# A fused attention and channel-mixing kernel: operands laid out on the host, channels on partitions, 512 tokens per matmul

## The chip, the cores and the metric

The kernel runs on one core of a Trainium2 chip. The metric is the device time of one execution in microseconds (us). The engines that the text names are TensorE (PE; its weight loads are listed as PEld), VectorE (DVE), ScalarE (ACT), GpSimd (POOL) and SyncE (SP), whose queue starts nearly all DMA transfers here. Each engine executes its own instructions in the order that was fixed when the kernel was compiled, and waits on semaphores for the others.

## The reference

All inputs are float32 or float64 arrays: q, k and v of shape (8 batches, 8 heads, 576 tokens, 64), and the matrices U (576 x 32), V (32 x 576), w1 (512 x 2048), w2 (2048 x 512), which are float64.

```python
scores = q @ k.T / 8                       # per batch and head, 576 x 576
local   = (0 <= i - j < 32)                # heads 0 to 3
strided = (i >= j) and (i % 32 == j % 32)  # heads 4 to 7
attn = softmax(where(mask, scores, -1e9))
x = concat over heads of attn @ v          # (8, 576, 512)
h = (x.transpose(0, 2, 1) @ U @ V).transpose(0, 2, 1)   # mixing over tokens
u = x + h
out = u + maximum(u @ w1, 0) @ w2          # (8, 576, 512)
```

A local head needs only a band of keys: for 32 queries the 64 keys up to them. A strided head splits into 32 residue classes of 18 tokens each.

## The kernel before

**The two large products.** Token rows of u are cut into 18 blocks of 256 tokens (two tiles of 128). For each block and each of 16 chunks `fc` of the 2048 hidden channels, `gemm1` (L714) forms the hidden activations with hidden channels on partitions and 256 tokens as columns: four slices of channels times three matmuls. Three, because every operand is split in a high and a low float32r part and the product of the two low parts is left out (high x high, high x low, low x high). ACT writes the high part of the ReLU (`gh`, L726) and DVE the low part (`gl`, L727). `gemm2` (L731), two steps later, takes the activations as the stationary operand and moves 512 output channels: for each of the two token tiles three matmuls, accumulated over all 16 chunks in two PSUM banks `acc`. `finish` (L742) adds u and stores token rows. One step, a pair (block, fc), is therefore 12 matmuls of 256 columns and 6 of 512.

**Weights.** w1 and w2 lie in memory as float64 bits. They are loaded as 32 chunks of 512 KB (`load_weights`, L146) and converted by integer operations (`to_f32`, L104: one on ACT, three on DVE, L114 to L117) and then split (ACT L164, POOL L165), during the front and the first two blocks, which run interleaved.

**Attention.** Batches 0 and 1 (`early`, `attention_pair`, L247) do all eight heads on TensorE: a pair of heads is loaded in its natural layout, transposed by TensorE, evicted by ACT and DVE (`transpose_natural`, L193; `copy`, L219), scored against 32-token chunks, masked by a matmul, exponentiated, transposed again and multiplied with v. The strided pairs reach their residue order through DRAM (`sd` for v, `od` for the output). Batch 1's pairs start while batch 0's are still running. Batches 2 to 7 do the local heads on TensorE (`local_pairs`, L452, with DVE 32x32 transposes, L464), and the strided heads with products on POOL and reductions on DVE (`strided_heads`, L480: L504 and L506 for the scores, L532 and L534 for the outputs), then ACT copies to token rows (`strided_copies`, L541).

**Mixing and transposition.** `mix_t` (L563) forms x^T U, `mix_u` (L589) adds the product with V to x. u is stored with tokens on partitions, so each block has to be turned to channels on partitions before `gemm1` (`transposes`, L675): the first three blocks by TensorE, the others by DVE 32x32 transposes and 16 DMA transfers of 32 KB.

**What sets the order.** The kernel is traced as Python generators. The loop at L792 walks the 288 steps and, after each, advances the generators of strided heads, of the next batch's attention and of the transposes by a fraction of their length that was chosen by hand (windows L759). Tile, the framework, then orders each engine's instructions at compile time: first traced is preferred, a later one may go ahead where an earlier one is not ready by its own estimate of times. Tiles of one tag share a fixed number of buffers: seven `att` buffers, one `st` (strided q, k, v), two PSUM pairs `px`, one pair `acc`, two banks `ph`.

Of the kernel before, what the change touches and what calls it, by code (L numbers as in the profile page):

```python
# [39 lines left out]
B1S, B1E = 24, 1  # L40
ORDER0, ORDER1 = (0, 2, 3, 1), (0, 2, 3, 1)
# [3 lines left out]
def fused_kernel(ctx, tc, q, k, v, U, V, w1_in, w2_in, masks, eye, out):  # L45
    nc = tc.nc
    B, H, S, D = q.shape
    DM, FF = w1_in.shape
    R = U.shape[1]
    NCH = S // 32  # L50
    NFC = FF // 128
    NDC = DM // 128
    NG = 4
    FPG = NFC // NG

    const = ctx.enter_context(tc.tile_pool(name="const", bufs=1))
    xp = ctx.enter_context(tc.tile_pool(name="xp", bufs=2))
    ap_ = ctx.enter_context(tc.tile_pool(name="ap", bufs=1))
    mp = ctx.enter_context(tc.tile_pool(name="mp", bufs=2))
    dp = ctx.enter_context(tc.tile_pool(name="dp", bufs=2, space=bass.MemoryType.DRAM))  # L60
    ps_acc = ctx.enter_context(tc.tile_pool(name="ps_acc", bufs=1, space=bass.MemoryType.PSUM))
    ps_h = ctx.enter_context(tc.tile_pool(name="ps_h", bufs=2, space=bass.MemoryType.PSUM))
    ps_x = ctx.enter_context(tc.tile_pool(name="ps_x", bufs=2, space=bass.MemoryType.PSUM))
# [4 lines left out]
    def big(shape, name, dtype=F32):  # L68
        return ap_.tile(shape, dtype, name=name, tag="big")

    def ubuf(shape, name, dtype=F32):
        return mp.tile(shape, dtype, name=name, tag="u", bufs=5)

    counts = {"xn": 0, "conv": 0}
    banks = {"n": 0, "prefix": True}

    def psx2():

        banks["n"] += 1
        if banks["prefix"] and banks["n"] % 3 == 0:  # L80
# [3 lines left out]
    def psx1():  # L84
        if banks["prefix"]:
            return ps_h.tile([128, 512], F32, name="ph")
        return psx2()[:, 0, :]
# [5 lines left out]

    ident = const.tile([128, 128], F32, name="ident")
    masks_sb = const.tile([128, 768], BF16, name="masks_sb")
    mask_b = masks_sb[:, 0:640].rearrange("p (a t x) -> p a t x", a=2, x=64)
    ident_b = masks_sb[:, 640:768]
    kZ = const.tile([128, 2, 32 + S], F32, name="kZ", tag="kZ")
    nc.vector.memset(kZ, 0.0)
    U_sb = const.tile([128, 5, R], F32, name="U_sb")  # L100
    Vst = const.tile([96, S], F32R, name="Vst")
    raws, w_parts = {}, {}

    def to_f32(raw, p, n, paced=False):  # L104
# [4 lines left out]
        cv = att([128, 512], "cv")  # L109
# [11 lines left out]
    def small_weights():  # L121
        stage = xp.tile([128, 2, 512], I64, name="xg")
        raw = stage[:, 0]
        dma(out=raw[:, 0:4 * R].rearrange("p (t r) -> p t r", r=R),
                          in_=U[0:512, :].rearrange("(t p) r -> p t r", p=128))
        for half in range(2):
            dma(out=raw[64 * half:64 * half + 64, 4 * R:5 * R], in_=U[512:576, :])
        rvs = []
        for a, n, s0 in ((0, 512, 0), (512, 64, 512)):
            rv = raw[0:32, 5 * R:5 * R + n] if n < 512 else stage[0:32, 1]  # L130
            dma(out=rv, in_=V[:, s0:s0 + n])
            rvs.append(rv)
        yield
        f = to_f32(raw, 128, 5 * R)
        nc.vector.tensor_copy(out=U_sb.rearrange("p t r -> p (t r)"), in_=f)
        yield
        for rv, (a, n) in zip(rvs, ((0, 512), (512, 64))):
            f = to_f32(rv, 32, n)
            nc.scalar.copy(out=Vst[0:32, a:a + n], in_=f)
            nc.scalar.copy(out=Vst[32:64, a:a + n], in_=f)  # L140
            nc.vector.tensor_tensor(out=Vst[64:96, a:a + n], in0=f, in1=Vst[0:32, a:a + n].bitcast(F32), op=ALU.subtract)
            yield

    chunks = [(i, g, t) for g in range(NG) for i in range(2) for t in range(4)]

    def load_weights():  # L146
        for i, g, t in chunks:
            src = w2_in[512 * g + 128 * t:512 * g + 128 * t + 128, :] if i else \
                w1_in[128 * t:128 * t + 128, 512 * g:512 * g + 512]
            raws[i, g, t] = const.tile([128, 512], I64, name=f"raw{i}_{g}_{t}", tag=f"w{i}_{g}_{t}")  # L150
            with tc.issue_after(last_dma[0]):
                nc.sync.dma_start(out=raws[i, g, t], in_=src)
            yield

    def weights():
        for n, (i, g, t) in enumerate(chunks):
            while wl["n"] <= n:
                next(wl["gen"])
                wl["n"] += 1
            f = to_f32(raws[i, g, t], 128, 512, True)  # L160
            parts = const.tile([128, 2, 512], F32R, name=f"w{i}_{g}_{t}", tag=f"w{i}_{g}_{t}")
            w_parts[i, g, t] = parts
            hi, lo = parts[:, 0], parts[:, 1]
            nc.scalar.copy(out=hi, in_=f)  # L164
            nc.gpsimd.tensor_tensor(out=lo, in0=f, in1=hi.bitcast(F32), op=ALU.subtract)  # L165
            yield

    wl = {"gen": load_weights(), "n": 0}

    def load_ahead(n):  # L170
        while wl["n"] < min(n, len(chunks)):
            next(wl["gen"])
            wl["n"] += 1

    xgs, tails, tsts, o_str = {}, {}, {}, {}

    xn_bufs = []

    def load_natural(src, h0):
        counts["xn"] += 1  # L180
        if counts["xn"] == 5:
            stage = xp.tile([128, 3, 640], F32, name="xg")
            xn_bufs.extend(stage[:, n] for n in range(3))
        if counts["xn"] <= 4:
            xn = ubuf([128, 640], "xn")
        else:
            xn = xn_bufs.pop() if xn_bufs else att([128, 640], "xn")
        rows = src[h0:h0 + 2].rearrange("h (j two) d -> (h j) (two d)", two=2)
        dma(out=xn[:, 0:512].rearrange("p (t x) -> p t x", t=4), in_=rows[0:512].rearrange("(t p) x -> p t x", p=128))
        dma(out=xn[0:64, 512:640], in_=rows[512:576])  # L190
        return xn

    def transpose_natural(dsts, xn, strided, engines):  # L193

        tp = psx2().rearrange("p a x -> p (a x)")
        for t in range(5):
            n = 128 if t < 4 else 64
            nc.tensor.transpose(out=tp[:, 128 * t:128 * t + n], in_=xn[0:n, 128 * t:128 * t + 128], identity=ident[0:n, 0:n])
        for hh in range(2):
            for par in range(2):  # L200
                src = tp[64 * par:64 * par + 64, 288 * hh:288 * hh + 288]
                if strided:
                    dst = dsts[hh].rearrange("p (j two i) -> p two i j", two=2, i=NCH)[:, par]
                    src = src.rearrange("p (i j) -> p i j", i=NCH)
                else:
                    dst = dsts[hh].rearrange("p (j two) -> p two j", two=2)[:, par]
                copy(engines[par], dst, src)
            yield

    def load_blocks(src, h0):  # L210
        xn = att([128, NCH, 32], "xn")
        for hh in range(2):
            sv = src[h0 + hh].rearrange("(c p) (e j) -> e p c j", p=32, e=2)
            for e in range(2):
                a = 64 * hh + 32 * e
                dma(out=xn[a:a + 32], in_=sv[e])
        return xn

    def copy(engine, out, in_):  # L219
        if engine == "a":  # L220
            nc.scalar.copy(out=out, in_=in_)  # L221
        else:
            (nc.vector if engine == "v" else nc.gpsimd).tensor_copy(out=out, in_=in_)  # L223

    halves = [slice(64 * hh, 64 * hh + 64) for hh in range(2)]

    held = {}
    vts, later_vt = [], []

    def acquire(names):  # L230

        while True:
            for name in names:
                if name not in held:
                    held[name] = True
                    return name
            yield

    def value_tiles():

        for vt in (big([128, NCH, 2, D + 1], "vt"), const.tile([128, NCH, 2, D + 1], F32, name="vt_kept")):
            nc.gpsimd.memset(vt, 0.0)
            for hh in range(2):
                nc.gpsimd.memset(vt[64 * hh:64 * hh + 64, :, hh, D:D + 1], 1.0)
            vts.append(vt)

    def attention_pair(b, pr, sd, od, last):  # L247


# [632 lines left out]
```

## Time and profile before

| | before |
|---|---|
| three runs, median (lowest to highest) | 1017.75 us (1016.87 to 1019.25) |
| profiled execution, its span | 1018.0 us |
| PE busy, share of the span | 961.5 us, 94% |
| DVE, ACT, POOL busy | 607.9, 312.1, 362.0 us |
| first matmul of `gemm1` | at 92.0 us |
| DMA moved, mean rate | 71.43 MB, 70 GB/s |
| packets under 512 B | 148952 of 186100 |

The span is the time from the first to the last instruction of one profiled execution. A line of a view names the source line, the engine, the operation and the tiles (`out<-in`); `x` counts instructions. In a timeline the first number is the start, the second the time to the end of the merged instructions, and brackets give the idle time before them with what ended it. In a group the busy time, the mean of one instruction in ns, and the idle time before it. Matmuls are pipelined: the duration of one (287 ns for 256 columns) is longer than the distance between two.

### The profile page before, as it was taken

The page shows a single profiled execution, that of the slowest core. Times are in us where ns is not written, and L with a number is a line of the kernel's source. Part 1 is how long each engine was busy: PE and PEld are TensorE (multiplying, and loading weights), DVE is VectorE, ACT ScalarE, POOL GpSimd, SP SyncE. Part 2 cuts the span into 40 slices and gives each one's busy share as a digit, 9 for nine tenths or more (in the row PEclk, how much of TensorE's full clock was granted, in tenths as well). Part 3 has the DMA queues.
Part 4 walks back from the last instruction along what each step waited for, and adds up shares of the span by engine and source line. Part 5 has one row for each costly group of instructions (what it writes and reads, how often), then busy time and mean ns, then how long its engine had stood idle before and what let it go on. Part 6 is the DMA issues. An engine that isn't in the chain of part 4 may idle for free.

```text
span 1018.0 us, 19929 instructions
## 1 busy us (share of the span) xinstructions
PE 961.5 (94%) x8028; PEld 835.2 (82%) x8028; DVE 607.9 (60%) x1137; ACT 312.1 (31%) x691; POOL 362.0 (36%) x376
## 2 busy tenths in 40 slices
PE   4666789999999999999999999999999999999997
PEld 3545678898788888988888888888888889999997
DVE  3546896888576847653758675858576843312121
ACT  6877445215211421211412142114211431211110
POOL 1102444965463517231455353735373500000000
PEclk9777799999999999999999999999999999999999
DMA  7866823052505250311251425042505300101000
GB/s 191 219 161 182 329 41 65 1 110 48 90 22 89 48 91 16 70 24 43 47 91 35 76 47 91 19 92 48 91 18 90 50 22 16 48 1 42 1 21 21
DMA packets 186100, 71.43 MB, mean 70 GB/s; under 512 B 148952, under 2 KB 177272, under 8 KB 186008
## 3 DMA queue, kind: packets, MB, share of 16 engines
q1 hardware_dynamic: 186008, 70.16, 31.9%
q8 instruction: 63, 1.03, 0.4%
q14 instruction: 29, 0.24, 0.1%
HBM read 51.64 MB, written 11.80 MB: 62 GB/s over the span
## 4 chain that ended last, share of the span: by engine, by line
PE 77%; DVE 8%; issue 5%; DMA 5%; SPq 2%; ACT 2%; POOL 1%; DVEq 0%; POOLq 0%; ACTq 0%
PE ph L722 36%; PE acc L739 33%; DMA raw<-in_moe_w_ch_dram 3%; SPq L92 2%; DVE st L534 1%; PE px L406 1%; PE px L739 1%; DVE cv L115 1%; DVE cv L117 1%; PE px L438 1%; DVE cv L114 1%; PE px L426 1%; DMA xn<-in_k_dram 1%; ACT qT L221 1%; PE px L596 1%
## 5 line engine op out<-in xcount | busy, mean ns | idle before, releaser
L722 PE MATMUL ph<-uh,w 128*128 128x256 f32 x2304 | 473.3, 287 | 10.9 <-DVE gl L727 5.9
L722 PEld LDWEIGHTS ph<-uh,w 128*128 128x128 f32 x2304 | 379.8, 191 | 27.0 <-DVE gl L727 8.7
L739 PE MATMUL acc<-w,gh 128*128 128x512 f32 x1088 | 346.5, 397 | 2.0 <-DVE qT L223 1.6
L722 PE MATMUL ph<-ul,w 128*128 128x256 f32 x1152 | 332.0, 288 | 0.0
L727 DVE SCALAR_TENSOR_TENSOR gl<-ph,gh 128x256 fp32r<-128x256 f32 x288 | 120.8, 420 | 253.8 <-ACT gh L726 252.5
L726 ACT ACTIVATE gh<-ph 128x256 fp32r<-128x256 f32 x288 | 110.1, 383 | 499.9 <-PE ph L722 440.1
L722 PEld LDWEIGHTS ph<-ul,w 128*128 128x128 f32 x1152 | 217.9, 189 | 9.9
L739 PEld LDWEIGHTS acc<-w,gh 128*128 128x128 f32 x1088 | 195.1, 189 | 34.4 <-issue 2.4
L532 POOL TENSOR_TENSOR tmp<-st,s_st 128x448 f32<-128x448 f32 (+7 forms) x162 | 139.0, 882 | 221.7 <-DMA st<-in_v_dram 79.7
L739 PE MATMUL acc<-w,gl 128*128 128x512 f32 x544 | 214.2, 394 | 0.0
L504 POOL TENSOR_TENSOR tmp<-st 128x576 f32<-128x576 f32 (+6 forms) x162 | 169.1, 1083 | 89.9 <-DMA vt<-in_v_dram 45.1
L534 DVE TENSOR_REDUCE st<-tmp 128x64 f32<-128x64 f32 (+8 forms) x162 | 136.9, 868 | 7.4 <-POOL tmp L532 5.8
L739 PEld LDWEIGHTS acc<-w,gl 128*128 128x128 f32 x544 | 102.9, 189 | 19.3
L506 DVE TENSOR_REDUCE s_st<-tmp 128x9 f32<-128x576 f32 (+6 forms) x162 | 87.6, 565 | 24.5 <-POOL tmp L504 23.9
L165 POOL TENSOR_TENSOR w<-cv,w 128x512 fp32r<-128x512 f32 x32 | 45.7, 1439 | 126.9 <-ACT w L164 109.6
L549 ACT COPY xg<-st 32x256 f32<-32x256 f32 x96 | 38.7, 404 | 32.2 <-DVE st L534 31.3
L709 DVE TENSOR_TENSOR ul<-u,uh 128x1024 fp32r<-128x1024 f32 x15 | 19.6, 1304 | 25.9 <-ACT uh L708 24.5
L114 DVE TENSOR_SCALAR cv<-cv 128x512 int32<-128x512 int32 (+3 forms) x35 | 19.8, 575 | 18.6 <-ACT cv L112 18.5
L581 DVE TENSOR_TENSOR ta<-px,ta 32x256 f32<-32x256 f32 x42 | 17.6, 420 | 19.9 <-ACT ta L579 18.8
L164 ACT CAST w<-cv 128x512 fp32r<-128x512 f32 x32 | 19.6, 618 | 32.0 <-DVE cv L117 30.2
L117 DVE SCALAR_TENSOR_TENSOR cv<-raw,cv 128x512 int32<-128x512 int32 x32 | 26.6, 836 | 0.3
L115 DVE SCALAR_TENSOR_TENSOR cv<-raw,cv 128x512 int32<-128x512 int32 x32 | 25.2, 796 | 0.3
(133 smaller groups left out, 632.6 us busy)
## 6 DMA issues: line engine op xcount, KB each, us to landing
raw<-in_moe_w_ch_dram SPq DMA_DIRECT2D x32, 512.0 KB, 8.5
out_dram<-xg SPq DMA_DIRECT2D x32, 256.0 KB, 2.2
u<-bt SPq DMA_DIRECT2D x240, 32.0 KB, 1.9
vt<-in_v_dram SPq DMA_DIRECT2D x28, 144.0 KB, 4.1
st<-in_q_dram SPq DMA_DIRECT2D x24, 144.0 KB, 3.8
st<-in_k_dram SPq DMA_DIRECT2D x24, 144.0 KB, 5.0
st<-in_v_dram SPq DMA_DIRECT2D x24, 144.0 KB, 3.1
xn<-in_k_dram SPq DMA_DIRECT2D x48, 72.0 KB, 2.5
```

The source lines that it names most:

```text
L115: nc.vector.scalar_tensor_tensor(out=i, in0=hi_w, scalar=-0x80000000, in1=i, op0=ALU.bitwise_and, op1=ALU.bitwise_or)
L117: nc.vector.scalar_tensor_tensor(out=i, in0=lo_w, scalar=29, in1=i, op0=ALU.logical_shift_right, op1=ALU.bitwise_or)
L165: nc.gpsimd.tensor_tensor(out=lo, in0=f, in1=hi.bitcast(F32), op=ALU.subtract)
L504: nc.gpsimd.tensor_tensor(out=tmp[:, 0:n], in0=sk[:, j0:j0 + n], in1=sq[:, i:i + 1].broadcast_to([128, n, D]), op=ALU.mult)
L506: late.append(lambda tmp=tmp, n=n, i=i, j0=j0: nc.vector.tensor_reduce(out=s_st[:, i, j0:j0 + n], in_=tmp[:, 0:n], axis=AX.X, op=ALU.add))
L532: nc.gpsimd.tensor_tensor(out=tv, in0=sv[:, 0:i + 1, d0:d0 + step], in1=s_st[:, i, 0:i + 1].broadcast_to([128, i + 1, step]), op=ALU.mult)
L534: late.append(lambda tv=tv, i=i, d0=d0, step=step: nc.vector.tensor_reduce(out=o_st[:, i, d0:d0 + step], in_=tv.rearrange("p j d -> p d j" ...
L549: nc.scalar.copy(out=xg[32 * i4:32 * i4 + 32, :, cs], in_=o_st[rows, i4:16:4, :])
L722: nc.tensor.matmul(ph[:, 0:W], w_parts[0, g, dc][:, part, fs], ut[:, :, :, dc, :], start=(dc == 0 and i == 0), stop=(dc == NDC - 1 and i = ...
L726: gate[:] = [nc.scalar.activation(out=gh[:, 0:W], in_=ph[:, 0:W], func=AF.Relu).ins]
L727: nc.vector.scalar_tensor_tensor(out=gl[:, 0:W], in0=ph[:, 0:W], scalar=0.0, in1=gh[:, 0:W].bitcast(F32), op0=ALU.max, op1=ALU.subtract)
L739: nc.tensor.matmul(accs[n][:, s, :], gt[:, cs], w_parts[1, g, f][:, part, :], start=(fc == 0 and i == 0), stop=(fc == NFC - 1 and i == 2))
```

## The change

The kernel is rewritten. Seen from its parts:

- **Host layout** (`_layouts`). q and k are given transposed (channels of a head pair on 128 partitions), v as overlapping windows with a column of ones, the strided heads of batches 0 and 1 already in residue order, those of the later batches with (head, residue) on 128 partitions, U padded in two orders, and every weight chunk contiguous. Weights stay float64 bits and are converted as before. The two early batches' strided heads, the `sd` and `od` tensors and the natural transposes are gone; all TensorE pairs use one `attention_pair`.
- **u with channels on partitions.** x keeps tokens on partitions (`x_loc`, `x_str`, one buffer each). `u_part` transposes x on TensorE into PSUM and adds the product with V there by accumulation (`tst` stationary, `Vst` moving), and `split` writes the high and low parts straight into `uh` and `ul` [128, 4, 512]. For strided heads of batches 2 to 7 DVE transposes the outputs instead. DVE and DMA transposes of u are gone.
- **Blocks of 512 tokens.** Nine blocks. `gemm1` moves 512 tokens; `gemm2` has w2 stationary and moves 512 tokens, so the output has channels on partitions, is stored so, and is turned on the host. Both have 12 matmuls of 512 columns per step, 144 steps.
- **Batches against blocks.** Block n holds the last 64n tokens of batch n-1 and the first 512-64n of batch n. `u_parts(b, 1)` writes batch b's part of block b, `u_parts(b, 2)` the rest into block b+1, whose buffer is that of block b-1. During block n: phase 2 of batch n at steps 2 and 3, strided heads and local pairs of batch n+1 at steps 4 to 12, the second mix and phase 1 of u at steps 13 and 14 (`stages_of`).
- **Buffers.** PSUM: `acc` two pairs, both used by each block, `ph` two banks, `px` one pair after the front (two before). `uh`, `ul` two each. `st` one, `att` seven as before, now also for the output tiles.
- **finish** adds `ul` on DVE and `uh` on POOL and stores 256 KB for each of four channel slices.
- **Front.** All four pairs of batch 0 are loaded first, with the first ten weight chunks between and behind; batch 1 starts in block 0, beside the conversion of the remaining weights, two chunks per step.

```diff
-    seq = sorted(((n, fc) for n in range(NLEAD) for fc in range(NFC)), key=lambda z: (z[1] + SKEW * z[0], z[0]))
-    seq += [(n, fc) for n in range(NLEAD, len(blocks)) for fc in range(NFC)]
...
+    def gemm1(n, fc):
+        g, f = fc // 4, fc % 4
+        uh, ul = uT[n]
+        ph = ps_h.tile([128, 512], F32, name="ph")
+        fs = slice(128 * f, 128 * f + 128)
+        for dc in range(NDC):
+            for i, (part, ut) in enumerate(((0, uh), (0, ul), (1, uh))):
+                nc.tensor.matmul(ph, w_parts[0, g, dc][:, part, fs], ut[:, dc, :],
+                                 start=(dc == 0 and i == 0), stop=(dc == NDC - 1 and i == 2))
...
+    def gemm2(n, fc, gh, gl):
...
+        for m in range(NDC):
+            ms = slice(128 * m, 128 * m + 128)
+            for i, (gt, part) in enumerate(((gh, 0), (gl, 0), (gh, 1))):
+                nc.tensor.matmul(accs[n][m // 2][:, m % 2], w_parts[1, g, f][:, part, ms], gt,
+                                 start=(fc == 0 and i == 0), stop=(fc == NFC - 1 and i == 2))
+
+    def finish(n):
+        uh, ul = uT[n]
+        for m in range(NDC):
+            o = att([128, TB], "o")
+            nc.vector.tensor_tensor(out=o, in0=accs[n][m // 2][:, m % 2], in1=ul[:, m].bitcast(F32), op=ALU.add)
+            nc.gpsimd.tensor_tensor(out=o, in0=o, in1=uh[:, m].bitcast(F32), op=ALU.add)
+            dma(out=out[m][:, TB * n:TB * n + TB], in_=o)
...
+    def split(n, dc, cols, src, engine, order=None):
+        uh, ul = (z[:, dc, cols] for z in block_u(n))
...
+        nc.scalar.copy(out=uh, in_=src)
+        engine.tensor_tensor(out=ul, in0=src, in1=uh.bitcast(F32), op=ALU.subtract)
...
+        if strided:
+            px = psx2()[:, 0, 0:hi - lo]
+            nc.tensor.matmul(px, tst, Vst[:, lo:hi], start=True, stop=True)
+            src = o_str[b][:, dc - 2, lo:hi]
+            nc.vector.tensor_tensor(out=src, in0=px, in1=src, op=ALU.add)
+            split(n, dc, cols, src, nc.gpsimd)
+            return
...
+        for s in range(base, top, 128):
+            w = min(128, top - s)
+            nc.tensor.matmul(px[:, s - base:s - base + w], x_loc[0:w, s // 128, 128 * dc:128 * dc + 128], ident[0:w, 0:w],
+                             is_transpose=True, start=(s - base) % 512 == 0, stop=False, skip_group_check=True)
...
+    def strided_heads(b):
+        st = ap_.tile([128, 2, NCH * D], F32, name="st", tag="st")
...
+        dma(out=st[:, 0], in_=sqkv[b - NSP, 0])
+        dma(out=st[:, 1], in_=sqkv[b - NSP, 1])
...
+    def stages_of(n):
+        b = n + 1
+        if b == 1:
+            return [Stage(u_parts(0, 2), 0, 0, 4), Stage(pairs_of(1), 1, 12, 36), Stage(rest_of(1), 13, 14, 4)]
+        found = [Stage(u_parts(n, 2), LAG, LAG + 1, 4)] if n < B else []
+        if b < B:
+            found += [Stage(strided_heads(b), LAG + 2, 12, 82), Stage(pairs_of(b), LAG + 2, 10, 24), Stage(rest_of(b), 13, 14, 7)]
+        return found
+
+    for n in range(NB):
+        stages = stages_of(n)
+        for fc in range(NFC):
+            if n == 0:
+                convert(needed(fc))
+            pend.append((n, fc) + gemm1(n, fc))
+            if n == 0:
+                load_weights(c0 + 8 + 3 * (fc + 1))
+                convert(max(c0 + 2 * (fc + 1), needed(min(fc + 2, NFC - 1))))
+            for s in stages:
+                s.run(fc)
+            if len(pend) > LAG:
+                item = pend.pop(0)
+                gemm2(*item)
+                if item[1] == NFC - 1:
+                    finish(item[0])
```

More of the change, by code (lines that the diff above doesn't have):

```diff
@@ L119, in to_f32 @@
         return f
-    def small_weights():
[L122 to L132, printed above, removed]
+    wl = {"loaded": 0, "conv": 0}
@@ new lines, in load_weights, with convert @@
+    def load_weights(n):
+        while wl["loaded"] < min(n, len(chunks)):
+            k = wl["loaded"]
+            c = chunks[k]
+            raws[c] = const.tile([128, 512], I64, name="raw%d_%d_%d" % c, tag=wtag(*c))
+            with tc.issue_after(last_dma[0]):
+                dma(out=raws[c], in_=wts[k])
+            wl["loaded"] += 1
+    def convert(n):
+        while wl["conv"] < min(n, len(chunks)):
+            k = wl["conv"]
+            load_weights(k + 1)
+            c = chunks[k]
+            f = to_f32(raws[c], 128, 512, True)
+            parts = const.tile([128, 2, 512], F32R, name="w%d_%d_%d" % c, tag=wtag(*c))
+            w_parts[c] = parts
+            nc.scalar.copy(out=parts[:, 0], in_=f)
+            nc.gpsimd.tensor_tensor(out=parts[:, 1], in0=f, in1=parts[:, 0].bitcast(F32), op=ALU.subtract)
+            wl["conv"] += 1
@@ L144, in fused_kernel @@
[L144 to L208, printed above, removed]
@@ new lines, in attention_pair @@
+        sp = scores(kT, qT, masks_sb[:, 320 * (pr // 2):320 * (pr // 2) + 320])
+        yield
+        s_sb = yield from probabilities(sp)
+        yield
+        yield
+        PT = transposed(s_sb)
+        yield
+        yield
+        op = outputs(PT, vt)
+        yield
+        normalised(op, pr)
+        yield
+    o_str = {}
+    def strided_heads(b):
+        st = ap_.tile([128, 2, NCH * D], F32, name="st", tag="st")
+        sq, sk = (st[:, x].rearrange("p (i d) -> p i d", d=D) for x in range(2))
+        dma(out=st[:, 0], in_=sqkv[b - NSP, 0])
+        dma(out=st[:, 1], in_=sqkv[b - NSP, 1])
@@ new lines, in first_attention, with load @@
+        late = [const.tile([128, 9, D + 1], F32, name=f"ve{n}", tag=wtag(n // 4, 3, n % 4)) for n in range(8)]
+        loads = {}
+        def load(k):
+            pr = PAIR_ORDER[k]
+            if k < 3:
+                qk = [scratch[j // 3][:, S * (j % 3):S * (j % 3) + S] for j in (2 * k, 2 * k + 1)]
+            else:
+                qk = [att([128, S], "kT"), att([128, S], "qT")]
+            loads[k] = pair_loads(0, pr, (*qk, late[2 * k], late[2 * k + 1]))
+        load(0)
+        dma(out=masks_sb, in_=masks)
@@ L731, in gemm2 @@
-    def gemm2(n, fc, gh, gl):
-        g, f = fc // FPG, fc % FPG
-        if fc == 0:
-            accs[n] = (ps_x.tile([128, 2, 512], F32, name="px") if 0 < n < NLEAD else
-                       ps_acc.tile([128, 2, 512], F32, name="acc"))
-        for s in range(len(blocks[n])):
-            cs = slice(128 * s, 128 * s + 128)
-            for i, (gt, part) in enumerate(((gh, 0), (gh, 1), (gl, 0))):
-                nc.tensor.matmul(accs[n][:, s, :], gt[:, cs], w_parts[1, g, f][:, part, :],
-                                 start=(fc == 0 and i == 0), stop=(fc == NFC - 1 and i == 2))
```

760 lines of the change are left out of this document (248 added, 512 removed).

## The prediction, made before the result was known

> **What bounds the kernel now.** I read the page first: span, engines, clock, the chain that ended last.
>
> ```profile
> span 1018.0 us, 19929 instructions
> PE 961.5 (94%) x8028; PEld 835.2 (82%) x8028; DVE 607.9 (60%) x1137; ACT 312.1 (31%) x691; POOL 362.0 (36%) x376
> PEclk9777799999999999999999999999999999999999
> PE 77%; DVE 8%; issue 5%; DMA 5%; SPq 2%; ACT 2%; POOL 1%; DVEq 0%; POOLq 0%; ACTq 0%
> ```
>
> TensorE is busy nearly everywhere, but the first four slices after the start have its clock at 7 tenths. So the kernel has two regimes, a front and a TensorE stream. The chain of waits in order of time dates the stream: the block marks, and two of its pieces with their counts.
>
> ```profile
> 273.16 2.96 PE acc L739 x12
> ...
> 482.98 1.45 PE ph L722 x12
> ...
> 883.45 3.17 PE acc L739 x14
> ...
> 901.68 1.81 PE acc L739 x8
> ...
> 928.46 3.17 PE acc L739 x14
> ...
> 1008.59 4.09 PE acc L739 x18
> ```
>
> A block of 256 tokens with nothing beside it takes 928.46 - 883.45 = 45.0 us. From 273.16 to 883.45, 12 blocks, it is 50.9: 5.9 more per block, and as a batch is 2.25 blocks, 13.2 us of side work on TensorE per batch. A 256-column matmul of the first product costs 1.45/12 = 0.121 us, a 512-column one of the second 1.81/8 = 0.226; from the block, (45.0/16 - 1.45)/6 = 0.227, which I use. The stream ends at 1012.7. The front ends at the first product's first matmul; batch 0's last pair is normalised long before.
>
> ```profile
> 59.05 0.69 DVE L366 TENSOR_TENSOR xg<-px,rt 128x512 f32<-128x512 f32 x1
> 91.98 0.50 PE L722 MATMUL ph<-uh,w 128*128 128x256 f32 x2 [1.54 <-ACT uh L691]
> 50.00:75.00 25.00, 16.38 (x222) 11.63 (x214) 11.92 (x28) 18.61 (x31) 2.52 (x2) 0.73 0.61 156
> 92.00:110.00 18.00, 12.71 (x70) 11.38 (x71) 12.92 (x24) 10.35 (x20) 3.74 (x3) 0.75 0.86 317
> ```
>
> (The two last rows are stretches: length, busy PE, PEld, DVE, ACT, POOL, then clock, DMA share, GB/s.) In 50 to 75 us ACT is the busiest engine, 18.6 of 25.
>
> **The change, part by part.** The sum is made against the profiled execution, 1018.0 us of span; the three runs have a median of 1017.75, so the two agree within 0.3 us and no correction is made.
>
> *Products.* 3456 matmuls of 256 columns become 1728 of 512; the second product keeps 1728 of 512. At 0.227 each a step (24 matmuls) is 5.45 us and a block of 512 tokens 87.2, nine of them 785 against 18 x 45.0 = 810: **-25 us**. Bounds: 0 if 512 columns cost twice 0.121 = 0.242; no gain beyond 25 has a row. I take 0.227, as it is the same type and width in the same array.
> [...]
>
> *Front.* Gone: natural transposes with four ACT evictions per tile, value copies, the two bounces through DRAM of the strided heads, and batch 1's pairs, which now run in block 0. Added: loads of 1.2 MB per pair in long rows; at the 317 GB/s of the row above, batch 0's four pairs, U, V, masks and two weight chunks (6.6 MB) land by about 25 us. Pair 3 then has its chain (scores, max, exp, transposes, outputs, normalise) of some 13 us, both mix products 5, the four parts of u 6 or more: the first product at **52 us**. Bounds: 42 (loads alone plus one chain) and 72 (pair 3 as late as the 59.05 above, plus 13). I take 52, nearer the low end, since ACT loses most of its work there.
>
> *Block 0.* TensorE: 87.2, and 20 more by estimate (13.2 for a batch as above, some 7 for its two further pairs and u's transposes): 107. DVE must convert some 25 weight chunks:
>
> ```profile
> L117 DVE SCALAR_TENSOR_TENSOR cv<-raw,cv 128x512 int32<-128x512 int32 x32 | 26.6, 836 | 0.3
> L115 DVE SCALAR_TENSOR_TENSOR cv<-raw,cv 128x512 int32<-128x512 int32 x32 | 25.2, 796 | 0.3
> L114 DVE TENSOR_SCALAR cv<-cv 128x512 int32<-128x512 int32 x32 | 19.0, 602 | 14.6 <-ACT cv L112 14.5
> L746 DVE TENSOR_TENSOR xg<-acc,xg 128x512 f32<-128x512 f32 x30 | 19.4, 682 | 5.3 <-PE acc L739 5.3
> ```
>
> 25 x 2.23 = 56, sixteen gl of 512 at about 0.68 = 11, pairs, mixes and u 21: 88, below TensorE. I take **110**; bounds 104 (13.2 and four) and 135 (a third of DVE's 88 not hidden). On SP the remaining weight chunks are issued ahead of batch 1's pairs; 22 x 0.5 MB and 4.8 MB at 317 GB/s are 51 us of transfer, under the 110.
>
> *Blocks 1 to 6.* TensorE: 87.2 + 13.2 + 1.6 (ten more transposes; five took 0.86, the first row below) = 102. The side chain is what changes its nature: within one block batch b+1 must pass finish, phase 2 of u (frees the single st buffer), load of q and k, POOL's products, load of v, POOL's second half, copies, mix, phase 1 of u. Before, 2.25 blocks of 45 us were there for it. Its pieces, from the timeline of each engine, the waits and the groups:
>
> ```profile
> 50.39 0.86 PE L198 MATMUL px<-ident,xn 128*128 128x128 f32 x5
> 617.81 1.93 SPq L92 DMA_DIRECT2D st<-in_q_dram  x4
> 621.30 0.64 PE L570 MATMUL px<-xg,U_sb 128*32 128x256 f32 x8
> 624.95 0.41 DVE L586 TENSOR_TENSOR tst<-ta,tst 32x256 fp32r<-32x256 f32 x1 [0.47 <-ACT tst L584]
> 626.80 17.22 POOL L504 TENSOR_TENSOR tmp<-st 128x64 f32<-128x64 f32 x19 [14.39 <-DMA st<-in_k_dram]
> 644.44 10.32 POOL L504 TENSOR_TENSOR tmp<-st 128x576 f32<-128x576 f32 x8 [0.42 <-DVE tst L586]
> 651.91 10.18 SPq L92 DMA_DIRECT2D u<-bt  x16
> 661.98 0.49 DVE L523 TENSOR_TENSOR s_st<-s_st,m_st 128x324 f32<-128x324 f32 x1
> 668.62 6.86 POOL L532 TENSOR_TENSOR tmp<-st,s_st 128x64 f32<-128x64 f32 x10 [13.85 <-DMA st<-in_v_dram]
> 711.93 1.16 POOL L532 TENSOR_TENSOR tmp<-st,s_st 128x576 f32<-128x576 f32 x1 [1.81 <-DVE st L534]
> 719.07 1.01 ACT L553 COPY xt<-st 32x64 f32<-32x64 f32 x4 [1.57 <-DVE st L534]
> POOL tmp L532 <- PE px L406: 67.7, 9, 32.7
> L532 POOL TENSOR_TENSOR tmp<-st,s_st 128x448 f32<-128x448 f32 (+7 forms) x162 | 139.0, 882 | 221.7 <-DMA st<-in_v_dram 79.7
> L165 POOL TENSOR_TENSOR w<-cv,w 128x512 fp32r<-128x512 f32 x32 | 45.7, 1439 | 126.9 <-ACT w L164 109.6
> ```
>
> - finish: 0.68 on DVE, then four adds on POOL at 1.44: 6.4.
> - phase 2 of u, four parts one after another through the one px buffer: about 7.
> - q and k: 9.0 before (617.81 to 626.80, eight issues of short rows); two issues now: about 7.
> - first half on POOL: 626.80 to 654.76, 28, unchanged.
> - v and softmax: 13.9 before; the softmax alone ended at 662.47, 7.7 after POOL. The load no longer stands behind sixteen small transfers (10.18 us of SP's issuing), so 7.7.
> - second half: 668.62 to 713.09, 44.5, with 67.7/6 = 11.3 per batch of waiting for buffers that local scores held. Those scores now come in the first half: 33 (bounds: 139.0/6 = 23 busy, 44.5).
> - last copies, 7.0 before (to 720.08); 3, as most run beside the second half.
> - mix 4.1 (621.30 to 625.36), four parts of u about 8: 12.
>
> Together L = 104 us from the second product's last matmul of block n-1 to u of block n+1. If TensorE were never late, that matmul would end 11 us into block n (two steps, as the products are two steps apart), and L would have 91. When u is late, the two remaining second products run in the gap, so each us of stall also starts the next chain earlier: block time P = 5.5 - (P - 102) + L, so P = (107.5 + L)/2 = 105.8. A stall of this size has a second price:
>
> ```profile
> 600.00:602.00 2.00, 0.59 (x5) 0.59 (x6) 1.97 (x3) 1.19 (x3) 1.02 (x1) 1.00 0.00 0
> 602.00:604.00 2.00, 2.00 (x58) 1.78 (x58) 1.91 (x5) 1.63 (x5) 1.12 (x2) 0.65 0.03 8
> 604.00:606.00 2.00, 2.00 (x28) 1.55 (x16) 1.79 (x4) 0.36 (x1) 1.49 (x2) 0.50 0.00 0
> ```
>
> After TensorE had been busy only 0.6 of 2 us its clock stood at 0.65 and 0.50 for 4 us: up to 1.7 us lost. I add 1.2: **P = 107**, six blocks 642. Bounds per block 102 (hidden) and 118 (below). What is covered only by TensorE's stream: the removed transposes of u through DVE and 240 small DMAs; they cost nothing before and save nothing now, except on SP's queue.
> [...]
>
> *Blocks 7 and 8, end.* 89 and 87: no attention left. Finish after the last matmul: one POOL add more than DVE can hide, 7.5 with the store, against 1018.0 - 1012.7 = 5.3 now.
>
> Sum: 52 + 110 + 642 + 89 + 87 + 7.5 = **988 us**, 3% faster: some 40 from the front, 25 from the products, given back in part by an attention chain that becomes the bound of six blocks.
>
> **The rivals.**
> 1. *The chain is hidden.* L below 96.5 (second half of POOL near its 23 busy): P = 102, 988 - 30 = 958. For it: DVE loses the 32-by-32 transposes. Against: POOL and DVE are equally loaded in that half, and gl stands in DVE's queue between the reductions.
> 2. *Slower: the chain keeps its old pace.* From the load's issue to the last copy it took 720.08 - 617.81 = 102.3 us; with finish, phase 2, mix and u, L = 102.3 + 13.4 + 12 = 128 and P = 117.7: 988 + 6 x 10.7 = 1052. It decides from P = 112, five us over mine. For it: one px and one st buffer, seven shared attention buffers in which POOL's products now also queue with the pair's; TensorE executes in its compiled order, so a mix placed too early stops the products behind it. Against: shorter loads, and scores no longer as fillers.
> 3. *The front stays.* First product at 72 or block 0 at 130, paced by weights: 988 + 20 = 1008. For it: DVE and DMA both carry batch 1 and the weights in block 0.
> 4. *The cadence does not improve:* 0.242 per matmul, 988 + 25 = 1013, the change not doing what it says.
>
> **How the numbers follow.** Forecast 0.45 (965 to 1010), hidden 0.25, old pace 0.18, front 0.07, cadence 0.05. The likeliest gives 988; the range from 950 (most of the hidden case) to 1048 (most of the old pace) leaves out 0.2. A measurement tells 0.2% (2 us) from no change. Slower by more: the old pace and tails of 3 and 4, 0.20; same 0.04; faster 0.76.
>
> **What would show it.** Right: first product near 52, its 512-column matmuls 0.227 apart, block marks about 107 apart for blocks 1 to 6 and 88 for the last two, a gap of TensorE once per such block behind mix or u with a drop of the clock, POOL's first half 28 us. Wrong: block marks of 102 with no gap, or 112 and more; a first product after 65; a block 0 ended by weights; matmuls at 0.24.

## The result, and the profile after

The changed kernel takes 988.73 us (median of 4 runs, 985.73 to 990.67) against 1018.41 us before on the same chip: ratio 0.9709, 95% interval 0.9683 to 0.9734. 988 was forecast. The terms behind it were further off than the total. The first rows of the page after:

```profile
span 988.9 us, 16540 instructions
PE 927.8 (94%) x6906; PEld 732.8 (74%) x6906; DVE 541.1 (55%) x942; ACT 252.4 (26%) x519; POOL 414.9 (42%) x433
PEclk7589988999999999999999999999999999999998
PE 67%; issue 10%; POOL 9%; DVE 9%; DMA 3%; ACT 2%; SPq 0%; POOLq 0%; ACTq 0%; DVEq 0%
```

The first matmul of a block's first product is called the block's mark. The stretches from mark to mark, in the columns of the prediction's stretches (length, busy PE, PEld, DVE, ACT, POOL, clock, DMA share, GB/s), are these; the last row is all of it, from block 0's mark to the last matmul:

```profile
51.34:177.90 126.56, 114.44 (x1037) 88.12 (x1038) 79.51 (x142) 48.77 (x89) 39.13 (x30) 0.90 0.20 69
177.90:282.10 104.20, 102.62 (x745) 80.22 (x744) 63.94 (x111) 28.25 (x61) 56.38 (x62) 0.98 0.15 51
282.10:384.40 102.30, 100.06 (x737) 79.18 (x737) 65.29 (x114) 26.49 (x59) 58.44 (x63) 1.00 0.15 52
384.40:486.80 102.40, 101.21 (x741) 79.49 (x739) 66.58 (x114) 26.56 (x59) 59.80 (x65) 1.00 0.15 52
486.80:591.70 104.90, 100.96 (x736) 79.93 (x736) 67.75 (x116) 26.50 (x59) 61.84 (x66) 0.98 0.16 56
591.70:697.00 105.30, 102.42 (x738) 81.29 (x738) 66.85 (x114) 26.51 (x59) 58.46 (x64) 0.97 0.15 51
697.00:801.60 104.60, 100.84 (x736) 79.94 (x736) 66.51 (x115) 26.51 (x59) 57.97 (x63) 0.98 0.13 45
801.60:888.60 87.00, 87.00 (x381) 71.26 (x382) 14.53 (x24) 12.46 (x23) 4.10 (x5) 0.98 0.02 7
888.60:981.20 92.60, 92.60 (x409) 76.36 (x407) 14.73 (x22) 9.57 (x16) 5.29 (x5) 1.00 0.03 12
51.34:981.20 929.86, 902.15 (x6253) 715.80 (x6253) 505.68 (x865) 231.61 (x484) 401.40 (x418) 0.98 0.13 45
```

| term | predicted | measured | difference |
|---|---|---|---|
| first product starts | 52 | 51.3 | -0.7 |
| block 0 | 110 | 126.6 | +16.6 |
| blocks 1 to 6 together | 642 | 623.7 | -18.3 |
| blocks 7 and 8 | 176 | 179.6 | +3.6 |
| tail | 7.5 | 7.7 | +0.2 |

Two errors of about 17 us cancel. Against the kernel before, the first product starts 40.7 us earlier (51.3 instead of 92.0), but the stretch from there to the last matmul is 9 us longer (929.9 instead of 920.7), and the tail 2.4: counted so, the whole gain is the front's, which no longer holds batch 1's pairs, and what the wider product saves is used up behind it.

Blocks 2 and 3 run at 102.3 and 102.4, the length that the rival "hidden" gave; blocks 4 to 6 at 105, each with the gap that was forecast. TensorE's timeline at the end of block 4, then the stretch of the gap and two behind it:

```profile
587.70 0.64 PE L318 MATMUL px<-x_str,U_sb 128*32 128x256 f32 x8
590.60 0.41 PE L389 MATMUL px<-ident,x_loc 128*128 128x128 f32 x2 [2.15 <-DVE ta L328]
591.72 1.22 PE L413 MATMUL ph<-uh,w 128*128 128x512 f32 x2 [0.59 <-ACT uh L349]
```

```profile
588.40:590.60 2.20, 0.05 (x4) 0.03 (x1) 1.96 (x5) 0.47 (x2) 2.20 (x3) 1.00 0.32 121
592.00:594.00 2.00, 2.00 (x6) 1.25 (x7) 0.81 (x2) 0.17 (x1) 0.17 (x1) 0.50 0.60 225
596.00:598.00 2.00, 2.00 (x6) 1.59 (x6) 0.36 (x1) 0.35 (x1) 0.59 (x1) 0.50 0.00 0
```

The batch's last mix has nothing of TensorE behind it, u's transposes wait 2.15 us for its additions, and the clock is at 0.50 for some 6 us. The strided heads' chain in the block from 486.8 has six pieces, one row each: POOL's first half; the softmax; POOL's second half; up to the first mix; to the next block's mark; and from that mark to the next batch's first product.

```profile
519.40:546.90 27.50, 27.50 (x258) 22.19 (x257) 18.80 (x35) 3.77 (x6) 27.50 (x27) 1.00 0.13 38
546.90:551.40 4.50, 4.50 (x22) 3.72 (x21) 4.28 (x12) 1.07 (x2) 0.04 (x1) 1.00 0.83 282
551.40:573.80 22.40, 22.40 (x209) 17.77 (x211) 21.01 (x29) 7.92 (x17) 22.38 (x27) 1.00 0.01 5
573.80:582.20 8.40, 8.40 (x78) 6.68 (x71) 8.06 (x13) 4.75 (x14) 0.39 (x2) 1.00 0.24 73
582.20:591.70 9.50, 6.78 (x56) 4.87 (x55) 6.56 (x13) 2.66 (x7) 4.48 (x4) 0.98 0.15 55
591.70:624.60 32.90, 32.88 (x135) 26.02 (x136) 8.30 (x15) 6.37 (x13) 3.67 (x5) 0.90 0.15 53
```

POOL is saturated in both halves, but has 3.7 us of work in the 33 us before the next batch's first product. What holds that product is the single st buffer: it is free only when the last part of u's second phase has been multiplied by TensorE (24.8 us behind the mark) and split by POOL; then comes the load.

```profile
616.48 0.34 PE L380 MATMUL px<-Vst,tst 96*128 96x384 f32 x1
618.45 1.01 POOL L350 TENSOR_TENSOR ul<-st,uh 128x384 fp32r<-128x384 f32 x1 [4.57 <-ACT uh L349]
619.49 0.81 SPq L57 DMA_DIRECT2D st<-in_sqkv_dram  x2
624.64 1.99 POOL L260 TENSOR_TENSOR tmp<-st 128x64 f32<-128x64 f32 x4 [5.18 <-DMA st<-in_sqkv_dram]
```

At the other end, the first mix is that of the local heads. Their last normalisation stands on VectorE behind the strided heads' last reductions and their transposition. The copies of the strided heads are done at 580.1, but their own mix comes only at 587.7, behind second products in TensorE's order:

```profile
576.73 2.35 DVE L288 TENSOR_REDUCE st<-tmp 128x32 f32<-128x576 f32 x2
579.11 1.01 ACT L307 COPY x_str<-st 32x64 f32<-32x64 f32 x4 [1.99 <-DVE st L288]
581.59 0.28 DVE L195 TENSOR_TENSOR x_loc<-px,rt 64x128 f32<-64x128 f32 x1
582.22 0.64 PE L318 MATMUL px<-x_loc,U_sb 128*32 128x256 f32 x8
```

### The profile page after: what moved, and what is told of

The parts are those of the page before. It is cut to its first block, busy times and chain, and to the rows that moved or that the text cites. A ratio compares the mean times of both kernels' runs of the same rounds, so it can differ in the third digit from the quotient of the medians.

```text
span 988.9 us, 16540 instructions
## 1 busy us (share of the span) xinstructions
PE 927.8 (94%) x6906; PEld 732.8 (74%) x6906; DVE 541.1 (55%) x942; ACT 252.4 (26%) x519; POOL 414.9 (42%) x433
## 4 chain that ended last, share of the span: by engine, by line
PE 67%; issue 10%; POOL 9%; DVE 9%; DMA 3%; ACT 2%; SPq 0%; POOLq 0%; ACTq 0%; DVEq 0%
PE acc L428 31%; PE ph L413 30%; POOL tmp L260 5%; DVE st L288 3%; POOL w L111 3%; DMA st<-in_sqkv_dram 1%; PE px L389 1%; DMA raw<-in_wts_dram 1%; PE px L149 1%; POOL tmp L286 1%; PE px L181 1%; PE px L318 1%; PE px L393 1%; DVE o L435 1%; PE px L170 1%
## 5 line engine op out<-in xcount | busy, mean ns | idle before, releaser
L413 PE MATMUL ph<-uh,w 128*128 128x512 f32 x1152 | 392.7, 401 | 6.7 <-ACT uh L349 5.0
L428 PE MATMUL acc<-gh,w 128*128 128x512 f32 x1152 | 383.9, 395 | 1.5 <-ACT w L110 1.3
L413 PEld LDWEIGHTS ph<-uh,w 128*128 128x128 f32 x1152 | 220.2, 193 | 56.7 <-ACT uh L349 7.8
L428 PEld LDWEIGHTS acc<-gh,w 128*128 128x128 f32 x1152 | 215.9, 189 | 48.4 <-ACT w L110 1.6
L413 PE MATMUL ph<-ul,w 128*128 128x512 f32 x576 | 231.5, 402 | 0.9 <-DVE ul L350 0.5
L428 PE MATMUL acc<-gl,w 128*128 128x512 f32 x576 | 226.2, 393 | 0.0
L418 DVE SCALAR_TENSOR_TENSOR gl<-ph,gh 128x512 fp32r<-128x512 f32 x144 | 98.3, 687 | 211.4 <-ACT gh L417 211.2
L417 ACT ACTIVATE gh<-ph 128x512 fp32r<-128x512 f32 x144 | 85.1, 597 | 419.2 <-PE ph L413 419.0
L413 PEld LDWEIGHTS ph<-ul,w 128*128 128x128 f32 x576 | 111.1, 193 | 25.4 <-DVE ul L350 1.4
L428 PEld LDWEIGHTS acc<-gl,w 128*128 128x128 f32 x576 | 108.4, 188 | 22.6
L350 POOL TENSOR_TENSOR ul<-st,uh 128x384 fp32r<-128x384 f32 (+7 forms) x24 | 19.2, 801 | 106.4 <-ACT uh L349 106.4
```

Source lines behind the costliest of these rows:

```text
L350: engine.tensor_tensor(out=ul, in0=src, in1=uh.bitcast(F32), op=ALU.subtract)
L413: nc.tensor.matmul(ph, w_parts[0, g, dc][:, part, fs], ut[:, dc, :], start=(dc == 0 and i == 0), stop=(dc == NDC - 1 and i == 2))
L417: gate[:] = [nc.scalar.activation(out=gh, in_=ph, func=AF.Relu).ins]
L418: nc.vector.scalar_tensor_tensor(out=gl, in0=ph, scalar=0.0, in1=gh.bitcast(F32), op0=ALU.max, op1=ALU.subtract)
L428: nc.tensor.matmul(accs[n][m // 2][:, m % 2], w_parts[1, g, f][:, part, ms], gt, start=(fc == 0 and i == 0), stop=(fc == NFC - 1 and i == 2))
```

## The experiments

Each edit is made on the changed kernel. Ratios are to the kernel before; lengths of blocks are read from one profiled execution of each. An edit in one place also changes the order that the compiler chooses elsewhere, so a block can move by some us for that reason alone: with first_256 below, blocks 2 and 3 take 111.5 and 97.2 us.

**Does the chain set blocks 4 to 6?** It was lengthened and shortened.

```diff
+                if i >= 9 and j0 == 0:                       # pool_longer
+                    more = att([128, 9, D], "more")
+                    nc.gpsimd.tensor_tensor(out=more, in0=sk[:, 0:9], in1=sq[:, i:i + 1]..., op=ALU.mult)
```

> Nine more POOL products of 128x576 per batch in the first half of the strided heads, about 1.1 us each, so the chain is some 10 us longer; their results are not used. Theory A (the chain's start hangs on TensorE's order of the same block, so a block is as long as the chain): blocks 4 to 6 go from 105 to about 115, and block 3 and 2 join them as the slack is gone earlier: kernel +30 to +45, about 1020 to 1035. The prediction's account (each us of stall also lets the next chain start earlier, half the slope): +5 per block, kernel about 1005. Rival, chain hidden: 989.

```diff
+                if i >= 9 and j0 == 0:                       # pool_shorter
+                    yield
+                    continue
```

> Nine of the 27 products of POOL's first half and their reductions are left out (scores of late chunks against the first nine), so the chain is some 10 us shorter. If the chain still sets blocks 4 to 6, they go to 102 or less and the gap before u's transposes is gone: 981 or less. If the order written at the end of a block sets them, they stay at 104 to 105 with the 2 us gap: 987 to 989.

One block of each, longer (1036.48 us, one run) and shorter (975.1 us, one run):

```profile
618.60:732.60 114.00, 101.75 (x737) 81.26 (x737) 66.16 (x113) 26.38 (x59) 70.87 (x73) 0.93 0.14 47
```

```profile
587.30:687.30 100.00, 99.50 (x737) 79.13 (x737) 58.83 (x104) 26.47 (x59) 46.00 (x54) 1.00 0.16 53
```

Blocks 4 to 6 average 104.9 us with 59.4 of POOL in the changed kernel. With 70.9 of POOL they take 114.6 (115.0, 114.0, 114.8); with 46.0 they take 100.0, the gap is gone and the clock is 1.00. So the chain binds these blocks, by 5 us; TensorE's own floor is 100, not 102; and the slope upwards is 9.7/11.5 = 0.84, not the half of the prediction. In the longer run POOL's first product still stands 32.4 us behind the mark (535.95 for 503.6), and TensorE's longest wait at a block's end, 6.1 us, is for the local heads' normalisation. In the shorter run blocks 2 and 3 became longer, 104.3 and 106.2 us, so only blocks 4 to 6 are read here.

```diff
-        found = [Stage(u_parts(n, 2), LAG, LAG + 1, 4)] if n < B else []
+        found = [Stage(u_parts(n, 2), LAG, LAG, 4)] if n < B else []      # u2_one_step
```

> All four parts of u's second phase are written in step 2 of a block instead of two in step 2 and two in step 3; nothing else changes. Theory A: in blocks 4 to 6 the strided heads' chain sets the pace, and its start hangs on TensorE's order, since the single st buffer is free only after the fourth part, which stands one step (5.4 us) behind the second. Then blocks 4 to 6 fall from about 105 to about 102, blocks 1 to 3 stay at 102 to 104, and the kernel gains 6 to 9 us: about 981. Rival B: the 2 us gap in front of u is the mix's own latency behind its px buffer and no chain ends there; the blocks stay at 105 and the kernel at 989.

989.79 us, ratio 0.9726 (0.9709 to 0.9743): nothing gained. The chain did start earlier:

```profile
619.24 2.83 POOL L260 TENSOR_TENSOR tmp<-st 128x64 f32<-128x64 f32 x5 [5.29 <-DMA st<-in_sqkv_dram]
...
683.03 0.64 PE L318 MATMUL px<-x_loc,U_sb 128*32 128x256 f32 x8
690.32 0.64 PE L318 MATMUL px<-x_str,U_sb 128*32 128x256 f32 x8
```

It now starts 28.5 us behind the mark (590.7) instead of 32.9, but the two mixes stand 7.3 us apart instead of 5.5, and blocks 4 to 6 take 103.8, 103.6 and 106.4. Rival B named the place; what POOL's first product gained, TensorE's compiled order gave back there.

```diff
+            yield from u_parts(b, 1, (0, 1))     # u_first, b >= NSP
             yield from mix_t(b, 1)
-        yield from u_parts(b, 1)
+            yield from u_parts(b, 1, (2, 3))
...
```

> For batches 2 to 7 the two parts of u that need only the first half of the mix are written ahead of the mix of the strided heads, the other two behind it. Theory: what is left at the end of blocks 4 to 6 is no longer the chain but the latency of that last mix (matmul, eviction, three additions, split) with nothing of TensorE behind it, 2.15 us plus up to 2 us of low clock; with two parts of u and six matmuls of the next block's first product to put there, blocks 4 to 6 fall from 105 to 102.5, the gap to under 1 us, the kernel to about 981. Rival: the strided heads themselves come too late, so that the mix is late by as much: blocks stay at 105, the gap moves to the third part of u; 989.

1001.78 us, ratio 0.9838 (0.9822 to 0.9855): 13 us slower than the changed kernel, which neither forecast had. The mix now queues behind two parts of u for px, and the wait comes back in front of the third part:

```profile
607.11 0.33 PE L380 MATMUL px<-Vst,tst 96*128 96x192 f32 x1 [2.39 <-DVE tst L335]
...
637.77 3.80 POOL L260 TENSOR_TENSOR tmp<-st 128x64 f32<-128x64 f32 x6 [5.48 <-DMA st<-in_sqkv_dram]
```

The strided parts of u come later, st is freed later, and the next batch starts 37.4 us behind its mark (600.4): blocks 4 and 5 take 106.

**What is the width of the first product worth?**

```diff
+                for x in range(2):                            # first_256
+                    cs = slice(256 * x, 256 * x + 256)
+                    nc.tensor.matmul(ph[:, cs], w_parts[0, g, dc][:, part, fs], ut[:, dc, cs], ...)
...
```

> The first product in two matmuls of 256 columns again instead of one of 512, all else as changed. By the prediction's durations (0.121 against 0.227 us) twelve products take 2.90 instead of 2.72: block 7, with nothing beside it, goes from 87.0 to 90, and the kernel to about 1010, a little less if the waits of blocks 4 to 6 absorb theirs. If only columns count, nothing changes: 989. [...]

992.95 us, ratio 0.9752 (0.9724 to 0.9779): 4 us slower than the changed kernel, not 21, and the two intervals overlap a little. Its block 0, its last block, and all blocks together:

```profile
50.90:168.60 117.70, 113.01 (x1229) 98.03 (x1229) 76.77 (x143) 48.85 (x89) 39.61 (x31) 0.95 0.22 76
887.50:983.10 95.60, 95.56 (x601) 86.37 (x599) 14.77 (x22) 9.57 (x16) 5.34 (x5) 1.00 0.03 12
50.90:983.10 932.20, 913.95 (x7981) 807.88 (x7981) 498.94 (x865) 230.72 (x484) 400.54 (x418) 0.99 0.13 46
```

In the last block, where TensorE waits for nothing, it costs 3.0 us (95.6 against 92.6). If each block costs as much, that is 27 over nine: the predicted 25 are there. The kernel does not show them because the other compiled order waits less: from the first mark on TensorE is idle for 18.3 us instead of 27.7, and its busy time grows by only 11.8, as less of it is spent at a low clock (mean 0.99 instead of 0.98). Block 0 takes 117.7 instead of 126.6.

**What makes block 0 long?** Its last third in the changed kernel, in VectorE's timeline, then TensorE's wait:

```profile
141.07 0.82 DVE L157 TENSOR_REDUCE mx<-px 128x10 f32<-128x640 f32 x1 [4.98 <-PE px L149]
...
149.71 4.07 DVE L85 SCALAR_TENSOR_TENSOR cv<-raw,cv 128x512 int32<-128x512 int32 x3
...
155.80 0.69 DVE L195 TENSOR_TENSOR x_loc<-px,rt 128x512 f32<-128x512 f32 x1
```

```profile
157.21 1.08 PE L318 MATMUL px<-x_str,U_sb 128*32 128x256 f32 x8 [4.67 <-DVE x_loc L195]
```

VectorE idles 5 us for the last pair's scores with conversions queued behind, then does them in a bunch, ahead of that pair's normalisation. Of the 12.1 us in which TensorE is idle in block 0, 8.9 lie between 140 and 160 us.

```diff
+        if paced and not banks["prefix"]:      # block0_no_int; the scale above it is 1.0 then
+            return f
```

> For the weight chunks that are converted after the first product has begun, the three integer operations of VectorE are left out, some 22 chunks x 2.2 us = 48 us (the weights are then wrong numbers of ordinary size). Theory A: block 0's 126.6 us come from VectorE's conversions standing ahead of batch 1's scores and normalisations; it falls to 112 or less, the idle time of TensorE from 12 to 4 us, and the kernel to about 974. Rival B: batch 1's pairs stand one behind the other for px and their values' buffer, whatever VectorE does: block 0 stays above 121. Rival C: the weights' loads end it: block 0 stays at 126.

980.31 us (one run); block 0 takes 117.7 us, between the forecasts of A and B. This does not show that the conversions account for the 9 us: first_256 keeps every one of them, has 3 us more of products, and its block 0 takes 117.7 as well, with the last pair's scores read by VectorE at 131.2 instead of 141.1. Another compiled order can be worth as much.

```diff
-            yield from run_staggered([attention_pair(b, pr) for pr in PAIR_ORDER], 6)
-            yield from mix_t(b, 1)
+            p = [attention_pair(b, pr) for pr in range(4)]       # block0_order
+            yield from run_staggered([p[2], p[3], p[0], mix_t(b, 1), p[1]], 5)
```

> Batch 1's pairs in block 0 run in the order 2, 3, 0, 1, five units apart instead of six, and the mix of the early strided heads stands ahead of the last pair instead of behind it. Theory: the last third of block 0 loses some 16 us because the last pair (scores at 140 us) and two mixes stand one behind the other; now one mix is off that row: the 4.7 us wait of the mix for the last normalisation goes, and as much of low clock: block 0 from 126.6 to about 118, kernel about 980. Rival: VectorE's conversions set it (they end at 155.7 us whatever the pairs do): 124 or more.

981.62 us, ratio 0.9635 (0.961 to 0.966). Block 0 takes 121.4 us, between the forecasts: the 4.7 us wait is gone, new waits for weights (1.5 and 2.8 us) take part of it.

```diff
-                load_weights(c0 + 8 + 3 * (fc + 1))
-                convert(max(c0 + 2 * (fc + 1), needed(...)))
+                load_weights(len(chunks))                  # weights_early
+                convert(max(c0 + 3 * (fc + 1), needed(...)))
```

> In block 0 the last weight chunks' loads are written in step 0, ahead of batch 1's value loads, which wait for their one buffer on the same queue (in the changed kernel four chunks are issued only at 95 us behind such a wait), and three chunks per step are converted instead of two; all else as changed. Theory: block 0's conversions end by 125 us instead of 156 and no longer bunch up with the last pair's normalisation: block 0 from 126.6 to 115 to 118, kernel about 978. Rival: the pairs' own row (px, values' buffer) sets the end of block 0: 123 or more.

985.2 us, ratio 0.9661 (0.9631 to 0.9692). Block 0 takes 121.3 us, between the forecasts. The conversions end at 136 instead of 156, and the last pair comes later (its scores at 150 instead of 140). Both draw on the seven attention buffers; that this is what delays the pair is likely, but no run shows it.

```diff
-        small_loads()                              # front_u_late: behind load(3); load_weights(2) gone
-            if i >= 3:          # U and V
+            if i >= 10:
-            if i >= 6 and i % 3 == 0:      # weights
+            if i >= 12 and i % 2 == 0:
```

> The loads of all four of batch 0's pairs go ahead of those of U, V and the weights, and U, V and the weights are converted only from the tenth turn of the front's loop. In the changed kernel ScalarE waits 10.2 us for U, with the exponentials of the third pair behind it in its queue. Theory: that wait, not the loads as a whole, delays the last pairs; the first product comes at 45 to 47 instead of 51. Then fewer chunks are converted before block 0, so some of it may come back there: kernel 984 to 990. Rival (the prediction's account: all loads land by 25 us, the last pair's chain of 13 us behind them): the first product stays at 50 to 52.

987.53 us (982.79 to 989.8), ratio 0.9693 (0.9661 to 0.9724), not told apart from the changed kernel. The first product starts at 48.9, between the forecasts: ScalarE's wait for U cost 2.4 us, not 5.

**Can the chain start earlier?**

```diff
-        xT = st[:, 1].rearrange("p (e s) -> p e s", e=2)
+        xT = ap_.tile([128, NCH * (D + 1)], F32, name="xT", tag="vt")[:, 0:NCH * D].rearrange(...)
-            found += [Stage(strided_heads(b), LAG + 2, 12, 82), ...
+            found += [Stage(strided_heads(b), 1, 12, 82), ...      # xt_own_buffer only
...
-            split(n, dc, cols, src, nc.gpsimd)
+            split(n, dc, cols, src, nc.vector)                     # xt_dve_block0, xt_dve_order
```

> The transposed output of the strided heads is written into the tile that holds the local pairs' values (idle at that time) instead of back into st, so st is free after the copies, and the strided heads are written from step 1 of a block instead of step 4; all the work is kept. In the changed kernel POOL's first product starts 33 us behind a block's first matmul, as st waits for the second phase of u, which has its place in TensorE's order of that block. Theory: this start makes the chain bind; the products start some 20 us earlier, the chain ends well ahead of the mix, and blocks 4 to 6 fall to TensorE's own 100 us, as they did with fewer products (100.0 to 100.1); kernel about 972 to 976. Rival: the end of a block (two mixes and u through one px buffer) or VectorE sets it: 103 or more, 984 to 989.

1013.72 us, ratio 0.9952 (0.9934 to 0.9969): 25 us slower than the changed kernel, which neither forecast had. The chain did start early, at 588.5, 21 us ahead of the mark (609.4). POOL's timeline behind that mark, and TensorE's wait:

```profile
617.97 3.35 POOL L260 TENSOR_TENSOR tmp<-st 128x384 f32<-128x384 f32 x3
621.28 1.26 POOL L436 TENSOR_TENSOR o<-o,uh 128x512 f32<-128x512 f32 x1
622.50 1.40 POOL L260 TENSOR_TENSOR tmp<-st 128x576 f32<-128x576 f32 x1
623.85 1.26 POOL L436 TENSOR_TENSOR o<-o,uh 128x512 f32<-128x512 f32 x1
625.07 0.59 POOL L350 TENSOR_TENSOR ul<-xT,uh 128x192 fp32r<-128x192 f32 x1
```

```profile
625.71 0.79 PE L413 MATMUL ph<-ul,w 128*128 128x512 f32 x1 [5.06 <-POOL ul L350]
```

The products that start earlier stand on POOL among the additions of finish and the splits of u for which the block's first product waits. So the split was moved to VectorE, which in the changed kernel has 8.3 us of work in the 33 behind a mark, and the strided heads were put back to step 4:

> Five edits that keep all the work. Blocks 1 to 6: the strided heads' transposed output has a tile of its own again (the idle values' tile), with the strided heads written from step 4 as in the changed kernel, and the split of u's strided parts is on VectorE instead of POOL, so that no product of POOL stands ahead of a split that TensorE waits for (the 5 us waits of xt_own_buffer). Block 0 and front: the edits of block0_order, weights_early and front_u_late together. Theory: a chain that starts about 25 us earlier is hidden once POOL is off TensorE's path; blocks 2 to 6 at 100 to 101.5 as in pool_shorter, block 0 at 115 to 119 with the front at 48 to 49: kernel 957 to 966. Rival 1: what xt_own_buffer lost was not POOL's queue but the later mixes (blocks at 105 to 108 again): 980 to 990. Rival 2: the three edits of block 0 get in each other's way in the ring of seven attention buffers: block 0 at 121 or more, 4 to 6 us above the first figure.

970.18 us, ratio 0.9542 (0.9526 to 0.9558). Blocks 2 to 6 fall to 100.0 to 100.2; block 0 takes 126.3, the length of rival 2, though no run shows that the seven buffers are the reason. With block 0's order edit alone:

> The two edits for blocks 1 to 6 of xt_dve_block0 (own tile for the transposed output, the split of u's strided parts on VectorE) with the order of block0_order in block 0 alone; front and weights as in the changed kernel. If the three edits of block 0 got in each other's way, as its 126.3 us suggest, then 50.4 (first product) + 121.4 (block 0) + 103 (block 1) + 5 x 100.1 + 86.6 + 92.6 + 7.7 = 962. Rival: block 0 is lengthened by the two edits of the later blocks (block 1's first work stands in its last steps): 126 again and 967.

962.8 us (961.45 to 963.79, 5 runs), ratio 0.9453 (0.944 to 0.9466): faster than both kernels, with all the work kept. Its block 0 and block 5, and POOL's first product in block 5, 3 us behind the mark instead of 33:

```profile
50.70:169.90 119.20, 112.04 (x1037) 86.18 (x1037) 80.60 (x144) 49.59 (x89) 41.90 (x31) 0.94 0.22 74
574.60:674.50 99.90, 99.42 (x738) 78.89 (x737) 67.77 (x118) 26.65 (x59) 55.94 (x59) 1.00 0.16 53
577.57 1.31 POOL L260 TENSOR_TENSOR tmp<-st 128x64 f32<-128x64 f32 x3
```

So a chain that starts 30 us earlier no longer binds. The own tile and the split on VectorE were only run together; what each is worth alone is not shown, nor what the place in step 1 instead of 4 cost xt_own_buffer.

## Why the prediction was right, and where it was not

The mechanism, a front that shrinks and an attention chain that becomes the bound, was right where it could be tested, in blocks 4 to 6. That the total came to within 1 us is luck: block 0 and blocks 1 to 6 were off by 17 and 18 us in opposite directions.

- **Front: right.** 51.3 for 52. The last pair's scores begin at 25.8 us and its values are normalised at 40.9, 15 us instead of 13; the mixes and u take another 10.4 instead of 11.
- **Products: right as work.** In block 8, where TensorE waits for nothing, 34 times 12 matmuls of 512 columns take 92.6 us, 2.72 each, and the width costs 3.0 us. As time it is worth 4 us, since waits fill what it frees.
- **Block 0: mis-sized by 17.** The step that failed is "88, below TensorE. I take 110": VectorE's 79.5 busy us fit by their sum, but not at their places. TensorE is idle for 12.1 us and loses about as much to a clock of 0.90 (0.10 x 126.6 = 12.7). Without both it would take 102 by this estimate, so the sum of TensorE's work, 107, was not too small.
- **Blocks 1 to 6: mechanism right for three, terms off.** In the cycle from 519.4 to 624.6 the chain's pieces compare as follows:

| piece | predicted | measured |
|---|---|---|
| mark to POOL's first product | 22.1 (5.5 - 3.8 of stall + 6.4 + 7 + 7) | 32.9 |
| first half | 28 | 27.5 |
| load of v and softmax | 7.7 | 4.5 |
| second half | 33 | 22.4 |
| up to the first mix | 3 | 8.4 |
| mixes and u, to the next mark | 12 | 9.5 |
| sum | 105.8 | 105.2 |

The second half is under its lower bound of 23: no wait for buffers was left. The start was not second product, finish, phase 2 in 7 us and load, but phase 2 at its place in TensorE's order, with its last part 24.8 us into the block. With the start tied to the mark, "each us of stall also starts the next chain earlier" falls. TensorE's floor is 100 instead of 102. The 105 of blocks 4 to 6 is near 107 because these errors offset. Blocks 2 and 3 live on the early start of batch 2, whose first product stands 13.5 us behind its mark; the next ones stand 19.8, 26.5 and 32.6 behind theirs, and by then the lead is used up.

- **Blocks 7 and 8: 3.6 short.** The two-step lag puts two second products of block 7 behind block 8's mark, so of the two blocks' 64 groups of 12 matmuls block 8 holds 34 and block 7 only 30, or 81.7 us. The other 5.3 of block 7's 87.0 are phase 2 of u and the low clock behind the last gap (0.80 from 801.6 to 804 us, 0.50 to 806, 0.89 to 808: a loss of 1.7), for which the prediction had 1.8 (89 - 87.2).
- **Rivals.** "Hidden" gave the length of blocks 2 and 3, though TensorE still stood 2 us above its own 100 there; it was true of blocks 2 to 6 in xt_dve_order. "Old pace" was too slow by 13 us a block: POOL's second half no longer waits. "The front stays" had block 0 at 130, paced by weights: it came to 126.6, with the conversions of weights and batch 1's pairs in each other's way.

What stays open: how much of block 0's excess is the conversions', the pairs' and the compiled order's, and how they can be untied together; three edits that each shortened block 0 alone (121.4, 121.3 and 123.5) gave 126.3 as one.

## What to carry to other kernels

Size a side chain by where its first instruction can stand in the bounding engine's order, not only by the sum of its pieces; and before starting it earlier, look at what stands behind it on its own engine. An engine that fits by its sum may still bind by its bursts: check the stretch in which its late work meets the last consumer. A gain of busy time on the bounding engine shows as time only where nothing else waits.

## What the runs showed of the hardware

In the gap shown above TensorE was busy for 0.86 of the 3.6 us from 588.4 to 592.0, idle for 2.15 and then 0.59 in one piece each, 2.7 together. Some 6 us at a clock of 0.50 followed (592 to 598), a loss of 3 us, about twice the 1.7 that the prediction read in the kernel before. In pool_longer TensorE was idle for 12.1 to 12.3 us of each of the three blocks 4 to 6, and they ran at a mean clock of 0.92 to 0.93.
